# The end of a fused attention and SwiGLU kernel: another order of the last products, halves with a bank each, and stores on two queues

## The chip, the cores and the metric

The kernel runs on one core of one Trainium2 chip. The metric is the device time of one execution in microseconds (us), the median of several runs. Below, TensorE is PE in the profile's rows (PEld its weight loads), VectorE is DVE, ScalarE is ACT, GpSimd is POOL and SyncE is SP; SPq and ACTq are the queues on which SP and ACT issue transfers.

## The reference, cut to what matters

Attention over 8 batches x 8 heads x 576 rows x 64 columns, in float32, with scores below the row's maximum less `tau` masked out, is followed by a SwiGLU block with 512 model columns and 1536 inner columns:

```python
scores = scale * np.matmul(q, k.transpose(0, 1, 3, 2))
thresh = np.max(scores, axis=-1, keepdims=True) - tau
scores = np.where(scores >= thresh, scores, -1000000000.0)
attn = softmax(scores)                       # with 1e-09 added to the sum
x = (attn @ v) as (B*S, H*D)                 # 4608 tokens x 512
g = x @ w_gate                               # 512 x 1536
silu = g * (1.0 / (1.0 + np.exp(-g)))
out = (silu * (x @ w_val)) @ w_out           # 1536 x 512
```

## The kernel before

**Chunks.** The tokens go through the SwiGLU block in chunks of 512. Chunk c, from 0 to 7, holds the first 512 rows of batch c; the 64 rows that are left of each of the 8 batches are gathered into a ninth chunk, c = 8, which the code calls `c == B`. While heads are still being attended, the products of a chunk lie between slots of attention. Chunks 7 and 8 come after the last attention (`tail[0]` is true), and nothing but their own work is left then.

**The output product of a chunk.** A chunk's 512 x 1536 activations times the 1536 x 512 matrix `w_out` is cut 2 x 2 x 2 and done by a scheme of the Strassen family with seven products of (256 x 768) by (768 x 256). Five of them, numbers 0, 1, 3, 5 and 6, are cut the same way once more: `nested` (L1297) issues seven smaller products of three matmuls each. Every float32 matmul stands twice in the profile, so a nested product is 42 matmul records; it lands in two PSUM banks called `px`. Products 4 and 2 are not cut: `flat` (L1314) issues two halves `i` of six matmuls, 24 records in all, both halves into one bank called `py`.

**The four output blocks.** The outcome is a block for each pair (t, e) of token half and column half. A block is 128 partitions x 512 float32 in SBUF, that is two halves `i` of 256 columns. `combine` (L1331) makes a block from a nested product with four DVE instructions. In before there are two places for blocks in the tile `whole`; `n = self.blocks % 2` picks one, and `combine` waits until the earlier store from that place has landed (`*ob_jobs[n]`, L1340). `ship` (L1357) stores a block. For chunk 8 it issues four transfers of 64 KB, all on SP (L1370), one for each half `i` and each 64 partitions `x`, since the rows of one batch are 64 rows of the output.

**The steps of a chunk in the tail** are listed by hand in `Deep.__init__` (L1251):

```python
self.steps = deque([self.p1, self.gates_end, self.p2, self.p7_alone, self.p5, self.p6_alone, self.p3, self.p4_alone])
```

- `p2` makes and ships block (0,0).
- `p7_alone` is nested product 6, copied to SBUF by ACT.
- `p5` is flat product 4. ACT copies its bank to SBUF (L1410), for `corner` needs it.
- `p6_alone` is nested product 5. DVE adds it to an earlier one (`add`, L1480 and L1482), combines what becomes block (0,1), adds `u3`, and `corner` makes and ships block (1,1).
- `p3` is flat product 2, added on top of product 4 in the same bank. One DVE instruction of 128x512 (L1423) adds the bank to block (0,1), which is then shipped.
- `p4_alone` is nested product 3. Two DVE instructions add it (L1480, L1482), `combine` makes block (1,0) from it, and it is shipped last.

**What orders the work around it.** PE's order is that of the calls. DVE, ACT, POOL and SP get their order from a planner (`Plan`): every job has a planned duration, jobs it waits for, and a rank; where several jobs of an engine could start, the lower rank goes first, then the one that was ready first. On the chip each engine runs that list in order. A job of rank 0 is taken ahead of others if it will be ready within 0.2 us. The DVE adds of products have rank 0; in the tail `combine` from SBUF, `u3` and `corner`'s add have rank 1. `take` picks PSUM banks; in the tail there are eight.

Of the kernel before, what the change touches and what calls it, by code (L numbers as in the profile page):

```python
# [14 lines left out]
ALU = mybir.AluOpType  # L15
# [12 lines left out]
class Plan:  # L28
# [12 lines left out]
    def job(self, eng, took, fn, *deps, rank=1, lag=0.0, moves=0.0):  # L41
        j = Job(eng, took, fn, rank, lag, moves)
        for d in deps:
            if isinstance(d, Job) and d.end is None:
                d.then.append(j)
                j.waits += 1
            elif d is not None:
                j.ready = max(j.ready, self.after(d, eng) if isinstance(d, Job) else d + self.HOP)
        if not j.waits:
            self.open[eng].append(j)  # L50
        return j
# [45 lines left out]
    def pe(self, took, fn, *deps):  # L97
        self.force(*deps)
        for d in deps:
            if d is not None:  # L100
                self.t = max(self.t, (d.end if isinstance(d, Job) else d) + self.HOP)
        self.run(self.t)
        fn()
        self.t += took
        return self.t + self.PIPE
# [7 lines left out]
def kernel(  # L113
# [11 lines left out]
    nc = tc.nc  # L125
    P = 128
    B, H, S, D = q.shape
    NP = H // 2
    DM, DFF = w_gate.shape
    NCC = DM // P  # L130
# [7 lines left out]
    SM = 512  # L138
# [4 lines left out]
    TC = 256  # L143
    NU = SM // TC
    BT = TC // (S - SM)
    NF2, DM2 = NF // 2, DM // 2
# [27 lines left out]
    HW = 2 * TC  # L174
# [7 lines left out]
    GW = NQ * HW  # L182
    OW = DM + P
# [586 lines left out]
    def take(name, full=False):  # L770
        free = [b for b in banks if (not b.held if b.fixed is not None else b.n in turns)]
        if full:
            free = [b for b in free if b.full]
            return Hold(min(free, key=Bank.free_at), name) if free else None
        n = sum(b.full for b in free)
        return Hold(min(free, key=lambda b: (b.full and n == 1, max(b.free_at(), plan.t))), name)
# [146 lines left out]
    class Group:  # L923
# [50 lines left out]
        def p6(self):  # L974
            u = self.u1_buf
            if self.b:
                m = self.mul(self.b, self.w[3], xs[1], False, self.cb, *self.w_deps[3], *ready_x[self.c][2])
            else:
                b = self.b = take("pb")
                m = self.mul(b, self.w[3], xs[1], True, *self.w_deps[3], *ready_x[self.c][2], *b.deps)  # L980
                m = job("DVE", 0.7, lambda: nc.vector.tensor_tensor(out=b.rows(), in0=b.rows(), in1=u.ap, op=ALU.add),
                        m, self.s1, rank=0)
                b.bank.full = True
            self.u1 = job("ACT", 0.55, lambda: nc.scalar.activation(u.ap, self.b.rows(), AF.Copy, scale=0.5), m, *self.u1_old, rank=0)
            if self.c >= DEEP and self.g + 2 < NF2:
                load_flow(self.c, self.g + 2, 0, plan.t + plan.PIPE)
# [87 lines left out]
                           (w12, w12, w11, ALU.subtract))[n]  # L1074
            summed.append(job("POOL", 1.3, pool_tt(o[:, fs], x[:, fs], y[:, fs], op), *deps, *summed[-1:], rank=2))

    ob_jobs = [[], []]
    o_of = lambda i, e: ob[:, i, e * DM2:(e + 1) * DM2]

    class Outputs:  # L1080
# [155 lines left out]
    class Deep:  # L1236


        def __init__(self, c, mark):
            self.c = c  # L1240
            halves = [hall[:, t].rearrange("p g f n -> p (g f) n") for t in range(2)]
            self.a11, self.a12, self.a21, self.a22 = (halves[t][:, k * NF2:(k + 1) * NF2] for t in range(2) for k in range(2))
            KW = NF2 * TC
            self.s2, self.s3 = (flow[:, lo:lo + KW].rearrange("p (f n) -> p f n", n=TC) for lo in (GW, GW - KW))
            self.place = flow[:, 0:KW]
            assert GW - KW >= 4 * HW
            self.ready = {}
            self.inner = {}
            self.blocks = 0
            if tail[0]:  # L1250
                self.steps = deque([self.p1, self.gates_end, self.p2, self.p7_alone, self.p5, self.p6_alone, self.p3, self.p4_alone])  # L1251
                self.spaces = [pall[:, n * CW:(n + 1) * CW] for n in range(5)]
            else:
                self.steps = deque([self.p1, self.gates_end, self.p2, self.p5, self.p6, self.p3, self.p7, self.p4])
                self.spaces = [*spaces, None, spaces[1]]
            self.ready["a11"] = [gated[c, 0, x] for x in range(NF2 // 2)]
            self.inner_sums(0, self.a11, self.place, self.ready["a11"], mark)
# [39 lines left out]
        def nested(self, o, holds, first, *deps):  # L1297
# [13 lines left out]
                m = pe(0.67, fn, *ready, *deps, *deep_jobs[o])  # L1311
            return m

        def flat(self, o, a, hold, first, *deps):  # L1314

            for i in range(2):
                def fn(i=i):
                    ps = hold.ap()[:, i * DM2:(i + 1) * DM2]
                    for f in range(NF2):
                        nc.tensor.matmul(ps, a[:, f, i * P:(i + 1) * P], operands[o][:, f, :], start=first and i == f == 0, stop=True,  # L1320
                                         skip_group_check=True)

                m = pe(NF2 * MM, fn, *deps)
            return m

        def copies(self, out, holds, *deps, rank=0):
# [3 lines left out]

        def combine(self, q, *deps, psum=False):  # L1331

            n = self.blocks % 2
            self.blocks += 1
            y = whole.rearrange("p (x q) -> p x q", q=P)
            x, free = n * OW // P, (DM, SPARE)[n] // P
            q0, q1 = (h.ap() for h in q) if psum else (q[:, 0:4 * P], q[:, 4 * P:CW])
            q0, q1 = q0.rearrange("p (x q) -> p x q", q=P), q1.rearrange("p (x q) -> p x q", q=P)
            one = q0[:, 0:1]
            deps = *deps, *ob_jobs[n]  # L1340
            if psum:
                one = y[:, free:free + 1]
                deps = [job("ACT", 0.28, lambda: nc.scalar.copy(one, q0[:, 0:1]), *deps, rank=0)]
                tt, eng, took, less, rank = dve_tt, "DVE", 0.42, 0.29, 0
            else:
                tt, eng, took, less, rank = (dve_tt, "DVE", 0.36, 0.23, 1) if tail[0] else (pool_tt, "POOL", 0.75, 0.44, 2)
            twice = lambda x: x.broadcast_to((P, 2, P))
            j = job(eng, took, tt(y[:, x:x + 2], twice(one), q0[:, 1:3], ALU.add), *deps, rank=rank)
            j = job(eng, took, tt(y[:, x + 3:free + 1:free - x - 3], twice(y[:, x + 1:x + 2]), q1[:, 1:3], ALU.add), j, rank=rank)
            j = job(eng, less, tt(y[:, x + 1], y[:, x + 3], q0[:, 3], ALU.add), j, rank=rank)  # L1350
            j = job(eng, took, tt(y[:, x + 2:x + 4], twice(y[:, free:free + 1]), q1[:, 0:2], ALU.add), j, rank=rank)
            return n, j

        def block(self, n):
            return obs[:, n * OW:n * OW + DM]

        def ship(self, t, e, n, j):  # L1357
            c = self.c
            o = self.block(n).rearrange("p (i n) -> p i n", i=2)
            cols = slice(e * DM2, (e + 1) * DM2)  # L1360

            def fn():
                if c < B:
                    at_ = c * S + t * TC
                    nc.sync.dma_start(out=out[at_:at_ + TC, cols].rearrange("(i p) n -> p i n", p=P), in_=o)
                else:
                    for i in range(2):
                        for x in range(2):
                            r = (t * BT + 2 * i + x) * S + SM
                            nc.sync.dma_start(out=out[r:r + D, cols], in_=o[x * D:(x + 1) * D, i])  # L1370

            ob_jobs[n] = [job("SP", 0.1, fn, j, lag=2.8)]

        def pair(self, name):
            holds = [take(name) for _ in range(2)]
# [30 lines left out]
        def p5(self):  # L1406
# [2 lines left out]
            t = self.spaces[4]  # L1409
            self.c5 = job("ACT", 0.57, lambda: nc.scalar.copy(t[:, 0:DM], y.ap()), m, *u_list[1].jobs, *u_list[2].jobs, *u_list[3].jobs, rank=0)  # L1410

        def p6(self):
            m = self.nested(5, self.x, False, *self.z)
            self.next_flow(0, 0, m)
            self.next_flow(1, 0, m, *self.ready["s4"])
            self.c6 = self.copies(self.spaces[2], self.x, m, *n_list[0].jobs, *n_list[1].jobs)
            self.n12, self.j12 = self.combine(self.spaces[2], *self.c6)
# [19 lines left out]
        def corner(self, t, *deps):  # L1437
            n, j = self.combine(t, *deps)
            o, s = self.block(n), self.spaces[4][:, 0:DM]
            tt, eng, took = (dve_tt, "DVE", 0.62) if tail[0] else (pool_tt, "POOL", 1.3)  # L1440
            j = job(eng, took, tt(o, o, s, ALU.add), j, self.c5, rank=1)
            self.ship(1, 1, n, j)
            for b in u_list:
                b.jobs = [*b.jobs, j]
# [420 lines left out]
```

## Time and profile before

| | us |
|---|---|
| median of 3 runs | 1388.4 (1386.22 to 1389.73) |
| the profiled execution's own time | 1387.66 |
| its span, from the first to the last instruction | 1385.9 |

The span is 1.8 us shorter than the profiled execution's own time, which is 0.7 us below the median of the runs. In the rows a number such as `x12` is a count of instructions; `out<-in` names the tiles written and read; a text in square brackets is the idle time of the engine just before and what ended it. The mean granted clock of TensorE was 0.997.

### The profile page before, as it was taken

How to read it: one execution, taken by the hardware profiler on the slowest of the kernel's cores; microseconds unless marked ns; L12 is line 12 of the kernel's file. 1: busy time of each engine (PE TensorE's matmuls, PEld its weight loads, DVE VectorE, ACT ScalarE, POOL GpSimd, SP SyncE). 2: the span in 40 equal slices, each digit the busy share in tenths (PEclk: the TensorE clock that was granted, in tenths of full speed). 3: DMA queues.
4: the chain of work that ended last, by engine and by line, in shares of the span. 5: the costliest groups of instructions: out<-in, count | busy, mean ns of one | idle time of the engine just before them, and what ended most of it. 6: DMA issues, size and time to landing. Idle time of an engine off the chain costs nothing.

```text
span 1385.9 us, 38809 instructions
## 1 busy us (share of the span) xinstructions
PE 1360.6 (98%) x15486; PEld 1115.8 (81%) x15486; DVE 1024.4 (74%) x2676; ACT 867.0 (63%) x2253; POOL 701.0 (51%) x649
## 2 busy tenths in 40 slices
PE   9998999999999999999999999999999999999997
PEld 6666787778778778878887788888888788899897
DVE  7978888887887776778678777887787764365364
ACT  6887766676756767677777766777677673221220
POOL 2456498844484669534973387427943591000000
PEclk9999999999999999999999999999999999999999
DMA  7834413465523541554154514542255304414411
GB/s 172 217 97 138 101 36 98 124 185 143 172 51 125 145 113 36 169 148 136 36 167 128 148 35 134 154 135 73 78 156 149 97 26 164 160 54 162 141 47 31
DMA packets 208388, 162.30 MB, mean 117 GB/s; under 512 B 166224, under 2 KB 180560, under 8 KB 202832
## 3 DMA queue, kind: packets, MB, share of 16 engines
q1 hardware_dynamic: 204608, 159.39, 40.6%
q8 instruction: 123, 2.02, 0.6%
q10 hardware_dynamic: 3600, 0.43, 0.2%
q14 instruction: 57, 0.47, 0.1%
HBM read 138.28 MB, written 21.50 MB: 115 GB/s over the span
## 4 chain that ended last, share of the span: by engine, by line
PE 90%; DVE 4%; ACT 2%; DMA 1%; SPq 1%; issue 1%; ACTq 0%; DVEq 0%
PE pb L940 17%; PE pa L940 12%; PE pe L940 12%; PE px L1308 12%; PE sc L1514 10%; PE xa L1611 9%; PE po L1106 5%; PE py L1320 5%; PE pg L1040 2%; PE pv L1040 2%; PE sc L940 1%; PE pv L517 1%; SPq L336 1%; DMA vall<-in_v_dram 1%; PE xa L500 1%
## 5 line engine op out<-in xcount | busy, mean ns | idle before, releaser
L1562 DVE SCALAR_TENSOR_TENSOR pall<-sc,th,pall 128x288 f32<-128x288 f32 x504 | 243.7, 514 | 63.7 <-ACT pall L1560 49.5
L940 PE MATMUL pb<-xall,big 128*128 128x256 f32 x1080 | 256.5, 380 | 0.0
L1560 ACT ACTIVATE pall<-sc,nm 128x288 f32<-128x288 f32 x504 | 231.9, 498 | 34.5 <-DVE pall L1562 34.2
L1590 DVE STREAM_TRANSPOSE pall<-pall 128x576 f32<-128x576 f32 x252 | 189.9, 765 | 59.3 <-ACT pall L1588 42.6
L940 PEld LDWEIGHTS pb<-xall,big 128*128 128x128 f32 x1080 | 203.7, 190 | 29.8 <-issue 2.2
L1588 ACT ACTIVATE pall<-pall,ri 128x288 f32<-128x288 f32 x408 | 186.6, 527 | 25.0 <-DVE ri L1576 24.3
L795 POOL TENSOR_TENSOR hall<-hall,tmp 128x512 f32<-128x512 f32 x80 | 103.7, 1296 | 160.1 <-DVE hall L993 144.7
L940 PE MATMUL pa<-xall,big 128*128 128x256 f32 x768 | 183.3, 381 | 0.0
L940 PE MATMUL pe<-xall,big 128*128 128x256 f32 x752 | 178.9, 381 | 0.0
L940 PEld LDWEIGHTS pa<-xall,big 128*128 128x128 f32 x768 | 144.0, 190 | 22.6 <-issue 2.7
L940 PEld LDWEIGHTS pe<-xall,big 128*128 128x128 f32 x752 | 141.9, 190 | 21.5 <-issue 2.7
L1514 PE MATMUL sc<-kT,qT 64*32 64x144 f32 (+1 forms) x5376 | 149.2, 345 | 2.9 <-DVE pall L1562 2.2
L1535 DVE TENSOR_REDUCE mx<-sc 128x2 f32<-128x576 f32 x168 | 124.7, 742 | 26.9 <-PE sc L1514 26.5
L1514 PEld LDWEIGHTS sc<-kT,qT 64*32 64x32 f32 x5376 | 97.8, 106 | 56.4 <-issue 20.2
L1611 PE MATMUL xa<-pall,vall 64*32 64x288 f32 x4032 | 132.3, 404 | 1.0 <-DVE hall L993 0.8
L1585 POOL TENSOR_SCALAR pall<-pall,ri 128x288 f32<-128x288 f32 x96 | 96.0, 1014 | 63.0 <-DVE ri L1576 62.9
L1611 PEld LDWEIGHTS xa<-pall,vall 64*32 64x32 f32 x4032 | 76.4, 107 | 50.1 <-issue 7.2
L1570 ACT COPY sums<-sums 32x6 f32<-32x6 f32 x336 | 66.6, 198 | 45.1 <-DVE pall L1562 40.5
L992 ACT ACTIVATE vall<-tmp 128x512 f32<-128x512 f32 x96 | 60.4, 629 | 52.6 <-DVE tmp L1005 29.9
L1549 ACT COPY mx<-mx 32x6 f32<-32x6 f32 x196 | 38.1, 194 | 61.3 <-DVE mx L1537 59.4
L1320 PE MATMUL py<-wo,hall 128*128 128x256 f32 x336 | 74.8, 379 | 0.0
L1537 DVE TENSOR_REDUCE mx<-sc 128x1 f32<-128x288 f32 x168 | 74.6, 444 | 0.0
(225 smaller groups left out, 2326.2 us busy)
## 6 DMA issues: line engine op xcount, KB each, us to landing
big<-sums_hbm SPq DMA_DIRECT2D x42, 1024.0 KB, 5.2
big<-sums_hbm SPq DMA_DIRECT2D x48, 768.0 KB, 4.7
vall<-in_v_dram SPq DMA_DIRECT2D x112, 144.0 KB, 3.1
out_dram<-big SPq DMA_DIRECT2D x32, 256.0 KB, 3.6
qT<-in_q_dram SPq DMA_DIRECT2D x112, 72.0 KB, 4.7
kT<-in_k_dram SPq DMA_DIRECT2D x112, 72.0 KB, 2.9
wo<-in_moe_w_gate_dram SPq DMA_DIRECT2D x16, 384.0 KB, 3.6
wo<-in_moe_w_val_dram SPq DMA_DIRECT2D x16, 384.0 KB, 4.6
```

The lines of the kernel that those rows point to most:

```text
L795: return lambda: nc.gpsimd.tensor_tensor(out=out, in0=a, in1=b, op=op)
L940: nc.tensor.matmul(ps[:, i], w[:, k_, i * P:(i + 1) * P], x[:, k_, :], start=first and i == k_ == 0, stop=True, skip_group_check=True)
L1308: nc.tensor.matmul(ps, a[:, f, :], ws[n][:, f, :], start=bank_ not in begun, stop=True, skip_group_check=True)
L1320: nc.tensor.matmul(ps, a[:, f, i * P:(i + 1) * P], operands[o][:, f, :], start=first and i == f == 0, stop=True, skip_group_check=True)
L1514: nc.tensor.matmul(pss[h][(slice(g * G, (g + 1) * G), *part)], qT[hs, col:col + G], kT[hs, c * SH + keys[0]:c * SH + keys[1]], start=True, ...
L1535: rs.append(job("DVE", 0.72, lambda n=n, tile_=tile_: nc.vector.tensor_reduce(out=mx[:, n:n + 2, 0], in_=tile_[:, :, 0:SH], axis=AX.X, op= ...
L1560: ej = job("ACT", 0.42, lambda x=x, n=n: nc.scalar.activation(ps[x], scs[x], AF.Exp, bias=nm[:, n:n + 1]), ej, *((masks[h, 0], masks[h, 1] ...
L1562: masks[x] = job("DVE", 0.45, lambda x=x, n=n: nc.vector.scalar_tensor_tensor(out=ps[x], in0=scs[x], scalar=th[:, n:n + 1], in1=ps[x], op0 ...
L1585: scaled.append(job("POOL", 1.02, lambda x=x, n=n: nc.gpsimd.tensor_scalar(out=x, in0=x, scalar1=ri[:, n:n + 1], scalar2=None, op0=ALU.mul ...
L1588: scaled.append(job("ACT", 0.46, lambda x=x, n=n: nc.scalar.activation(x, x, AF.Copy, scale=ri[:, n:n + 1]), rj, rank=rank))
L1590: seg["turned"].append(job("DVE", 0.72, lambda both=both: nc.vector.transpose(out=both, in_=both), *scaled, rank=rank))
L1611: nc.tensor.matmul(holds[a].ap()[x * G:(x + 1) * G, 0:SH].rearrange("d (i q) -> d i q", q=G), vr[rs, h, j, ds], p[rs, h, :, j, :], start=( ...
```

## The change

It concerns chunk 8 alone. The last two steps change places and form: flat product 2, `p3`, now comes last, after `p4_alone`. Both flat products of this chunk are issued as two halves, each half `i` with a PSUM bank of its own (`p5_end`, `p3_end`); ACT copies each half of product 4 by itself, and after product 2 DVE adds and ships each half by itself. Blocks get four places instead of two; the new two lie in the part of `whole` that earlier held streamed weights. A block is stored by two transfers, one for each 64 partitions, one on SP's queue and one on ACT's; the last block has two such pairs, one for each half.

```diff
-    ob_jobs = [[], []]
+    END = (OB + 2 * NCC * DFF + 2 * 3 * HW - GW + NF2 * TC) // P
+    AT_OUT = (0, DM // P), (OW // P, SPARE // P), (END, END + DM // P), (END + OW // P, END + (OW + DM) // P)
+    ob_jobs = [[] for _ in AT_OUT]
...
+                if c == B:
+                    self.steps = deque([self.p1, self.gates_end, self.p2, self.p7_alone, self.p5_end, self.p6_alone, self.p4_alone, self.p3_end])
...
+        def flat_half(self, o, a, i, ps, first, *deps):
+            def fn():
+                for f in range(NF2):
+                    nc.tensor.matmul(ps(), a[:, f, i * P:(i + 1) * P], operands[o][:, f, :], start=first and f == 0, stop=True,
+                                     skip_group_check=True)
+
+            return pe(NF2 * MM, fn, *deps)
...
-            n = self.blocks % 2
+            n = self.blocks % (len(AT_OUT) if self.c == B else 2)
             self.blocks += 1
             y = whole.rearrange("p (x q) -> p x q", q=P)
-            x, free = n * OW // P, (DM, SPARE)[n] // P
+            x, free = AT_OUT[n]
...
         def ship(self, t, e, n, j):
             c = self.c
             o = self.block(n).rearrange("p (i n) -> p i n", i=2)
             cols = slice(e * DM2, (e + 1) * DM2)
+            if c == B:
+                self.ship_end(t, cols, n, o, slice(0, 2), j)
+                return
...
-                    for i in range(2):
-                        for x in range(2):
-                            r = (t * BT + 2 * i + x) * S + SM
-                            nc.sync.dma_start(out=out[r:r + D, cols], in_=o[x * D:(x + 1) * D, i])
...
+        def ship_end(self, t, cols, n, o, i, j):
+
+            ob_jobs[n] = []
+            for x, (eng, queue) in enumerate((("SP", nc.sync), ("ACT", nc.scalar))):
+                to = out.rearrange("(b s) n -> s b n", s=S)[SM:S, t * BT + x:(t + 1) * BT:2, cols]
+                ob_jobs[n].append(job(eng, 0.6, lambda x=x, queue=queue, to=to: queue.dma_start(
+                    out=to[:, i], in_=o[x * D:(x + 1) * D, i]), j, lag=2.0, rank=0))
...
+        def p5_end(self):
+            self.ys = [take("py") for _ in range(2)]
+            t = self.spaces[4]
+            self.c5 = []
+            for i, y in enumerate(self.ys):
+                m = self.flat_half(4, self.a21, i, lambda y=y: y.ap()[:, 0:DM2], True, *y.deps, *self.ready["s1"])
+                self.c5.append(job("ACT", 0.36, lambda i=i, y=y: nc.scalar.copy(t[:, i * DM2:(i + 1) * DM2], y.ap()[:, 0:DM2]),
+                                   m, *u_list[1].jobs, *u_list[2].jobs, *u_list[3].jobs, rank=0))
+
+        def p3_end(self):
+            o = self.block(self.n12).rearrange("p (i n) -> p i n", i=2)
+            for i, y in enumerate(self.ys):
+                m = self.flat_half(2, self.a12, i, lambda y=y: y.ap()[:, 0:DM2], False, self.c5[i], *self.ready["s4"])
+                j = job("DVE", 0.4, lambda i=i, y=y: nc.vector.tensor_tensor(out=o[:, i], in0=y.ap()[:, 0:DM2], in1=o[:, i], op=ALU.add),
+                        m, self.j12, rank=0)
+                self.ship_end(0, slice(DM2, DM), self.n12, o, slice(i, i + 1), j)
+                y.read_by(j)
+                y.done(True)
```

More of the change, by code (lines that the diff above doesn't have):

```diff
@@ L1075, in output_sums @@
             summed.append(job("POOL", 1.3, pool_tt(o[:, fs], x[:, fs], y[:, fs], op), *deps, *summed[-1:], rank=2))
-    ob_jobs = [[], []]
+    END = (OB + 2 * NCC * DFF + 2 * 3 * HW - GW + NF2 * TC) // P
+    AT_OUT = (0, DM // P), (OW // P, SPARE // P), (END, END + DM // P), (END + OW // P, END + (OW + DM) // P)
+    assert NF2 * TC + 2 * OW <= GW and NF2 * TC % P == GW % P == 0
+    ob_jobs = [[] for _ in AT_OUT]
     o_of = lambda i, e: ob[:, i, e * DM2:(e + 1) * DM2]
@@ L1312, in nested @@
             return m
+        def flat_half(self, o, a, i, ps, first, *deps):
[4 more added lines that the diff above has]
+            return pe(NF2 * MM, fn, *deps)
         def flat(self, o, a, hold, first, *deps):
             for i in range(2):
[L1317 to L1323, printed above, removed]
+                m = self.flat_half(o, a, i, lambda i=i: hold.ap()[:, i * DM2:(i + 1) * DM2], first and i == 0, *deps)
             return m
@@ L1354, in block @@
         def block(self, n):
-            return obs[:, n * OW:n * OW + DM]
+            return whole[:, AT_OUT[n][0] * P:AT_OUT[n][0] * P + DM]
         def ship(self, t, e, n, j):
@@ L1360, in ship @@
             cols = slice(e * DM2, (e + 1) * DM2)
+            if c == B:
+                self.ship_end(t, cols, n, o, slice(0, 2), j)
+                return
             def fn():
[L1363 to L1366, printed above, removed]
-                    for i in range(2):
-                        for x in range(2):
-                            r = (t * BT + 2 * i + x) * S + SM
-                            nc.sync.dma_start(out=out[r:r + D, cols], in_=o[x * D:(x + 1) * D, i])
-            ob_jobs[n] = [job("SP", 0.1, fn, j, lag=2.8)]
+                at_ = c * S + t * TC
+                nc.sync.dma_start(out=out[at_:at_ + TC, cols].rearrange("(i p) n -> p i n", p=P), in_=o)
+            ob_jobs[n] = [job("SP", 0.1, fn, j, lag=2.8)]
+        def ship_end(self, t, cols, n, o, i, j):
[4 more added lines that the diff above has]
+                    out=to[:, i], in_=o[x * D:(x + 1) * D, i]), j, lag=2.0, rank=0))
         def pair(self, name):
@@ L1440, in corner @@
             tt, eng, took = (dve_tt, "DVE", 0.62) if tail[0] else (pool_tt, "POOL", 1.3)
-            j = job(eng, took, tt(o, o, s, ALU.add), j, self.c5, rank=1)
+            j = job(eng, took, tt(o, o, s, ALU.add), j, *(self.c5 if self.c == B else [self.c5]), rank=1)
             self.ship(1, 1, n, j)
```

## The prediction

> **What bounds the kernel now.** I read the page first. TensorE is busy for 98% of the span and carries 90% of the chain of work that ended last; its clock digits are nines throughout.
>
> ```profile
> span 1385.9 us, 38809 instructions
> PE 1360.6 (98%) x15486; PEld 1115.8 (81%) x15486; DVE 1024.4 (74%) x2676; ACT 867.0 (63%) x2253; POOL 701.0 (51%) x649
> PE 90%; DVE 4%; ACT 2%; DMA 1%; SPq 1%; issue 1%; ACTq 0%; DVEq 0%
> ```
>
> So the kernel's time is PE's work plus what comes after PE's last product. The change removes no matmul, so only that tail can give anything. The second view is busy time by stretch, with the cuts put where products begin and end (columns: length, PE, PEld, DVE, ACT, POOL, clock, DMA share, GB/s).
>
> ```profile
> 1362.90:1367.60 4.70, 4.70 (x44) 4.70 (x43) 0.00 (x0) 0.59 (x1) 0.00 (x0) 1.00 0.00 0
> 1367.60:1372.70 5.10, 5.10 (x26) 4.51 (x25) 4.80 (x12) 0.00 (x0) 0.00 (x0) 1.00 0.01 3
> 1372.70:1377.60 4.90, 4.89 (x43) 4.67 (x42) 1.15 (x2) 0.00 (x0) 0.00 (x0) 1.00 0.30 68
> 1377.60:1380.50 2.90, 0.00 (x0) 0.00 (x0) 2.20 (x5) 0.00 (x0) 0.00 (x0) 1.00 0.30 66
> 1380.50:1383.00 2.50, 0.00 (x0) 0.00 (x0) 0.42 (x1) 0.00 (x0) 0.00 (x0) 0.50 0.25 57
> 1383.00:1386.00 3.00, 0.00 (x0) 0.00 (x0) 0.00 (x0) 0.00 (x0) 0.00 (x0) 0.50 0.19 43
> ```
>
> To be seen: the last three products (nested 5, flat 2, nested 3) fill PE without a hole up to 1377.6, and then 8.3 us pass without a matmul. ACT does nothing after its copy at 1363. The third view is the timeline of DVE in that tail, the fourth that of SP.
>
> ```profile
> 1377.63 0.69 DVE L1480 TENSOR_TENSOR pall<-px,pall 128x512 f32<-128x512 f32 x1 [3.78 <-PE px L1308]
> 1378.24 0.55 DVE L1482 TENSOR_TENSOR pall<-px,pall 128x384 f32<-128x384 f32 x1
> 1378.70 0.42 DVE L798 TENSOR_TENSOR big<-pall 128x256 f32<-128x256 f32 x1
> 1379.75 1.21 DVE L798 TENSOR_TENSOR big<-big,pall 128x256 f32<-128x256 f32 x3 [0.63 <-DMA out_dram<-big]
> ```
>
> ```profile
> 1380.53 2.38 SPq L1370 DMA_DIRECT2D out_dram<-big  x4
> ```
>
> And of line 1370, the stores of chunk 8, from 1378 on:
>
> ```profile
> L1370 SPq DMA_DIRECT2D out_dram<-big x5: 466/594/596, 1377.6 to 1382.3; - x5
> DMA to landing us min/median/max: 1.9/2.0/2.1
> ```
>
> The 8.3 us are then: 2.90 us from the last product to the first of four stores (two adds, a combine, and 0.63 us in which the combine waits for the store of the block that had its place); 1.8 us until the fourth store is issued at 1382.3, since each takes SP about 0.6; 2.05 us until it lands at about 1384.35; and 1.55 us from there to the end of the span, which is the program's closing and no step of the change touches it. The chain of waits says why the place was late:
>
> ```profile
> 1376.98 0.59 SPq L1370
> 1377.58 0.04 issue
> 1377.62 2.05 DMA out_dram<-big
> 1379.67 0.03 DVEq L798
> ```
>
> Eight stores had queued on SP from 1373.28 (two blocks became ready together), the last went out at 1377.62 and landed at 1379.67.
>
> **The change part by part.** All sums are made against the profiled span of 1385.9.
>
> *Order on PE.* Nested 5, nested 3, flat 2 instead of nested 5, flat 2, nested 3. A nested product is 42 records at 0.112 us, 4.69; a flat one 24 at 0.216, 5.18. Nested 5 starts at 1362.87; nested 3 would then run from 1367.56 to 1372.25 and flat 2 from there, its last matmul starting at 1377.21 and lasting 0.38: 1377.59, as now. Moving costs nothing if the moved product's inputs are early. Nested 3's inner sums end on DVE at 1360.1, 7.4 us before it starts; flat 2 needs ACT's copies of product 4 (the bank was copied at 1363.07) and sums that ended by 1358. Its banks: two `px` are held by nested 5 until DVE has read them (1368.9), two by the `py` halves, which leaves four of eight. If the planner nevertheless gave nested 3 the banks of nested 5, PE would stand until 1368.9, 1.35 us; I take zero.
>
> *After the last product.* Two adds and a four-instruction combine are replaced by one DVE add of 128x256. Rows of that form read 0.42. It starts at 1377.63 and ends at 1378.05; the queues follow a DVE end by 0.03. Half 1 goes out at 1378.08, so 1380.53 - 1378.08 = 2.45 us are gained here, of which 0.63 is the wait for a place.
>
> *The stores.* The last block's second half is two transfers of 64 KB, issued at the same moment by SP and ACT. The three issues that stood before the last store, 1382.3 - 1380.53 = 1.8, are gone. Queued ahead on SP and ACT are block (1,1), ready near 1375, half 0 near 1375.5 and block (1,0) near 1376.6, one issue each of about 0.6: free by 1377.2. An issue of 128 KB (two runs of 1 KB per partition) is in no row of line 1370; the full-chunk stores of 256 KB on SP (L1365) took 0.41, so 0.6 is a safe value; 1.5 us, not seen on this queue, would be needed to hold up half 1.
>
> *What ACT's queue costs.* ACT has issued no transfer since 6.6 us. Its rows there stand beside SP's of the same form: k at 3.2 and 2.7 us to landing on ACTq, 2.8 and 2.5 on SPq, q at 2.9 and 3.1 against 3.2 and 2.6. Thus 0.2 to 0.5 slower at worst. ACT's in-order list has nothing behind these stores that PE or DVE waits for: the first one, of block (0,0) at 1355, has its 0.5 us before the copies at 1357.89, and after the copies of product 4 ACT has nothing but stores.
>
> *A rule against it.* A store of 64 KB lands in 2.0 us, and in the traffic of one such store the DMA digits stand at 9 for 0.3 to 0.4 us: one store fills the engines for that long. The Trainium skill (DMA: Bandwidth & Descriptors, Rules for kernel authors) says not to split a transfer into two over disjoint halves of the partitions, as they go over the same engines and run one after the other. By the row alone the pair lands in 2.05, by the rule in 2.05 + 0.4. I take 2.25 between them. The same page (Issuing engines are not separate DMA queues) adds that several issuers save only issue time, usually small; here issue time is 1.8 of the 8.3 us, so that this rule is no objection to the sum.
>
> *DVE before the end.* After nested 3 (1372.25) DVE still has the last combine step and the add of block (1,1), 1.1; nested 3's two adds, 1.24; its combine, 1.55; half 0's add, 0.42. That is 4.3 us, with hops 4.5, so done near 1376.8, and half 1 is due at 1377.63. So 0.8 us of cover. Were it gone, each us more would show in the end. The split makes two DVE adds of 0.42 from one of 0.68 and two ACT copies of 0.37 from one of 0.59, both hidden under PE. Without the two banks the add of half 0 would have to wait for PE to leave the bank; its store would then be a second one at the end.
>
> *The sum.* 1378.08 + 2.25 + 1.55 = 1381.9 against 1385.9: 4.0 us less. With landing at 2.05 it is 4.2; with 2.6 (rule, and ACT slower by 0.15) it is 3.65. The closing waits on eight transfer semaphores one after another, which may move it by 0.1 either way. The profiled execution (1387.66) is 0.7 below the median shown, and a difference carries over: 1388.4 - 4.0 = **1384.4**.
>
> **The rivals.** *Hidden collisions (part of the gain lost).* PE stands 1.35 us for a bank, or block (1,0) is combined after half 1 has come due and its 256 KB of stores are still in the engines. For it: DVE has only 0.8 us of cover, and two blocks and a half leave within 3.5 us, where before there was one at a time. Against: the bank count, and four stores of before in a row still landed in 2.0 each. It gives 4.0 - 1.35 to 4.0 - 2.0: 1385.8 to 1386.4.
>
> *The new places make waits of their own (the change does not do what it says).* With two places, block (1,0) in the new order would fall on block (0,1), which is not finished then; so the order needs more places, and the new ones overlay streamed weights. If block (1,1) or (1,0) waited there for something, DVE would be held. Against: chunk 8 loads no further weights, and the last product that reads them ends by 1348.5, some 20 us before the first write. A wait of up to 0.8 us would still be covered; one like that of before (0.63) costs nothing, and the time is 1384.4 again.
>
> *Slower: the ACT queue lands late.* Half of the last bytes now depends on a queue that has been idle for 1370 us. Were its landing not 2.25 but above 6.25 us, the whole gain is lost; the longest landing in the trace is 7.3 us (768 KB of weights under full traffic), and at that value the time is 1388.4 - 4.0 + 5.05 = 1389.5. To be slower by 0.3% it needs 10.4. Against: ACTq's own rows of 2.7 to 3.4, and idle engines at the end. I see no reason for it.
>
> **How the numbers follow.** About 0.3% (4.2 us) is what a measurement of this kernel can tell from no change, and my sum lies on that line. The sum as it stands: 0.72. Collisions: 0.20. Slower by the ACT queue or by something not seen: 0.05. Faster than the sum (closing shorter, landing at 2.0): 0.03, inside the range. The runs of before lie 3.5 us apart, so a median of such runs can stray by 1 to 1.5. Range: from 1388.4 - 4.4 - 1.5 = 1382.5 up to the collisions' 1386.4 with 0.6 of scatter, 1387.0. Faster by over 0.3%: somewhat over half of the main case, for its known uncertain terms (closing, landing) lean to the short side, and a little of the others: 0.55. Within: 0.40. Slower: 0.05.
>
> **What would show it.** In the profile after: PE busy to 1377.6 and no later; one DVE add of 128x256 as the last DVE instruction, near 1378.05; the last SPq and ACTq stores start together near 1378.1; landing of the last pair 2.0 to 2.6; no DVE wait on a store; block (1,0)'s stores issued before 1377. A span near 1381.9. Wrong would be: PE idle between nested 5 and nested 3; half 1's add starting later than 0.1 us after PE's end; stores of the last pair landing later than 3 us; or anything that differs before 1354, where the two programs are the same.

## The result and the profile after

The changed kernel took 1383.35 us (median of 6 runs, 1382.15 to 1383.97) against 1388.83 us before (6 runs); the ratio of the two is 0.9963, with a 95% interval of 0.9950 to 0.9976. In a second measurement it was 0.9967 (0.9954 to 0.9979). So it is faster, by about 0.35% (0.2 to 0.5% by the intervals). The profiled execution took 1383.97 us, its span was 1382.1.

Of the page of the changed kernel, the lines that answer to those of before:

```profile
span 1382.1 us, 38805 instructions
PE 1360.9 (98%) x15486; PEld 1115.3 (81%) x15486; DVE 1024.5 (74%) x2677; ACT 867.6 (63%) x2254; POOL 701.2 (51%) x649
PE 91%; DVE 4%; ACT 2%; SPq 1%; DMA 1%; issue 1%; ACTq 0%; DVEq 0%
```

PE does the same work in the same busy time, within 0.3 us. What changed is what follows it. Rows of the timeline of the changed kernel over its last ten microseconds (start, length, engine, line, what it is, and in brackets the idle time before it with what ended it):

```profile
1373.08 5.35 PE L1322 MATMUL py<-wo,hall 128*128 128x256 f32 x24
1375.73 3.67 SPq L1383 DMA_DIRECT2D out_dram<-big  x4
1375.74 3.69 ACTq L1383 DMA_DIRECT2D out_dram<-big  x4
1375.87 0.42 DVE L1437 TENSOR_TENSOR big<-py,big 128x256 f32<-128x256 f32 x1 [0.17 <-PE py L1322]
1376.21 1.20 DVE L798 TENSOR_TENSOR big<-big,pall 128x256 f32<-128x256 f32 x3
1378.46 0.42 DVE L1437 TENSOR_TENSOR big<-py,big 128x256 f32<-128x256 f32 x1 [1.05 <-PE py L1322]
```

The flat product is now last. DVE adds its first half at 1375.87, while PE still works on the second, then finishes block (1,0), and stands idle for 1.05 us before the second half is ready. One add of 0.42 us is all that is left after PE. The last pair of stores, in a narrower window of the same timeline:

```profile
1378.91 0.49 SPq L1383 DMA_DIRECT2D out_dram<-big  x1
1378.92 0.51 ACTq L1383 DMA_DIRECT2D out_dram<-big  x1
```

And the rows of line 1383 from 1378.5 on, with their time to landing:

```profile
L1383 SPq DMA_DIRECT2D out_dram<-big x1: 490/490/490, 1378.9 to 1378.9; - x1
L1383 ACTq DMA_DIRECT2D out_dram<-big x1: 506/506/506, 1378.9 to 1378.9; - x1
DMA to landing us min/median/max: 2.0/2.1/2.2
```

Below, the **tail** of a kernel is the time from the start of the DVE add that waits for the last product to the end of the span: before 1385.88 - 1377.63 = 8.25 us, after 1382.10 - 1378.46 = 3.64 us. It is 4.6 us shorter, although the span is only 3.8 us shorter: DVE's add, and with it the end of PE's work, lies 0.83 us later in this execution than in that of before. That has nothing to do with the change. The two programs are alike up to 1354, and the last product ahead of that, the last one of the SwiGLU gates, is late by as much already. Its row before, and its row after:

```profile
1346.58 1.89 PE L940 MATMUL sc<-xall,big 128*128 128x256 f32 x8
1347.41 1.89 PE L940 MATMUL sc<-xall,big 128*128 128x256 f32 x8
```

From there to the add it is 31.05 us in both, and in every other trace too, but for 31.2 in three parts (below). Of the 0.83 us, 0.29 stem from the transfer that brings `tau` in: it ended DVE's first wait at 5.50 us here and at 5.21 there. Where the rest arose was not looked for. The add starts anywhere from 1376.1 to 1379.6 us in the executions profiled here. This is why the tail, and not the span, is compared below. The 4.6 us are 2.45 from the end of PE's work to the first of the last stores, 1.79 of issues on SP, and 0.55 of the closing after the last landing, less 0.16 for a later landing.

### The profile page after: what moved, and what is told of

Its sections match the earlier page's. It is cut to its first block, busy times and chain, and to the rows that moved or that the text cites. A ratio compares the mean times of both kernels' runs of the same rounds, so it can differ in the third digit from the quotient of the medians.

```text
span 1382.1 us, 38805 instructions
## 1 busy us (share of the span) xinstructions
PE 1360.9 (98%) x15486; PEld 1115.3 (81%) x15486; DVE 1024.5 (74%) x2677; ACT 867.6 (63%) x2254; POOL 701.2 (51%) x649
## 4 chain that ended last, share of the span: by engine, by line
PE 91%; DVE 4%; ACT 2%; SPq 1%; DMA 1%; issue 1%; ACTq 0%; DVEq 0%
PE pb L940 17%; PE pa L940 12%; PE pe L940 12%; PE px L1313 12%; PE sc L1545 10%; PE xa L1642 9%; PE po L1109 5%; PE py L1322 5%; PE pg L1040 2%; PE pv L1040 2%; PE sc L940 1%; PE pv L517 1%; SPq L336 1%; PE xa L500 1%; PE sc L1313 1%
```

## The experiments

The question was which of the parts (order, halves with a bank each, two queues, four places) earns how much, and whether the parts add up. The theory was: the late combine, the wait for a place and the series of issues on SP are separate terms of the tail. The rivals were: one part carries it all, or two stores side by side gain nothing, since they go over the same engines.

**Two queues alone.** The kernel before, with this in `ship` for chunk 8:

```diff
+            if c == B:
+                for x, (eng, queue) in enumerate((("SP", nc.sync), ("ACT", nc.scalar))):
...
+                        out=to, in_=o[x * D:(x + 1) * D]), j, lag=2.0, rank=0))
```

> The kernel before, with only the stores of chunk 8 changed to two a block, one on SP's queue and one on ACT's; old order, one bank, two places. I read the tail: from the start of the DVE add that waits for the last product to the end of the span, 8.25 us before and 3.6 after. Theory (the series of issues and the late combine are separate terms): the issues, 1.8, go; the queue is no longer backed up, so the block's place is free in time and the 0.63 of waiting goes as well, although there are still two places; the last pair has 256 KB and lands some 0.6 later than 64 KB did. Tail 5.7 to 6.3, about 2.2 us less. Rival (the pair runs one after the other on the same engines, so nothing but issue time is saved, and the wait for the place stays): 6.9 or more. Rival (the stores are the whole gain, the order adds nothing): tail 3.6 to 4.2.

Measured: ratio 0.9995 (0.9987 to 1.0004). Its timeline at the end:

```profile
1379.64 0.69 DVE L1482 TENSOR_TENSOR pall<-px,pall 128x512 f32<-128x512 f32 x1 [3.78 <-PE px L1308]
1380.25 0.55 DVE L1484 TENSOR_TENSOR pall<-px,pall 128x384 f32<-128x384 f32 x1
1380.71 0.41 DVE L798 TENSOR_TENSOR big<-pall 128x256 f32<-128x256 f32 x1
1381.16 1.21 DVE L798 TENSOR_TENSOR big<-big,pall 128x256 f32<-128x256 f32 x3
1382.40 0.60 SPq L1366 DMA_DIRECT2D out_dram<-big  x1
1382.40 0.64 ACTq L1366 DMA_DIRECT2D out_dram<-big  x1
```

The wait on a store is gone from DVE, with two places, as the theory had it: the stores of the earlier blocks left in time. But the tail is 1386.31 - 1379.64 = 6.67 us, more than expected. The terms that the theory names, 8.25 - 1.8 - 0.63 + 0.6, come to 6.4 already, so its range was too low. One thing had been left out: a pair carries both halves of a block, and so waits for the last DVE step (until 1382.37), where the first of the four stores of before needed only one half and left 0.43 us ahead of that step's end. And ACT's half of a pair of 256 KB landed after 2.9 us in the two earlier pairs of this run, 0.2 more than allowed (the landing of the last one is not in the trace; SP's took 2.5). Against that, the closing was some 0.4 us shorter; the section on the prediction comes back to this. The rival of 6.9 is nearer to this number than the theory, but its wait for a place is refuted.

**Places alone.** The kernel before, with `AT_OUT` and four places:

```diff
-            n = self.blocks % 2
+            n = self.blocks % (len(AT_OUT) if self.c == B else 2)
-            x, free = n * OW // P, (DM, SPARE)[n] // P
+            x, free = AT_OUT[n]
```

> The kernel before, with only four places for the blocks of chunk 8 instead of two. Theory: the wait of 0.63 us of the last combine for its place goes and nothing else: tail 7.6 instead of 8.25; SP's queue is empty again by 1378.2, before the first store at 1379.9, so that the gain is not lost there. Rival (the store queue only takes the wait over): 8.25. In the times 0.6 us cannot be told from nothing.

Measured: ratio 0.9996 (0.9987 to 1.0005), tail 1384.51 - 1376.87 = 7.64. The timeline:

```profile
1376.87 0.69 DVE L1483 TENSOR_TENSOR pall<-px,pall 128x512 f32<-128x512 f32 x1 [3.78 <-PE px L1311]
1377.95 0.41 DVE L798 TENSOR_TENSOR big<-pall 128x256 f32<-128x256 f32 x1
1378.40 1.21 DVE L798 TENSOR_TENSOR big<-big,pall 128x256 f32<-128x256 f32 x3
```

No bracket stands behind the last row: the wait is gone, the tail is 0.61 us shorter, and nothing took the wait's place.

**Order alone.** The changed kernel with `p5` and `p3` whole, as before, and four stores a block on SP. It keeps the four places, which the new order needs:

```diff
-... self.p5_end, self.p6_alone, self.p4_alone, self.p3_end])
+... self.p5, self.p6_alone, self.p4_alone, self.p3])
...
+                for i in range(2):
+                    for x in range(2):
+                        nc.sync.dma_start(out=out[r:r + D, cols], in_=o[x * D:(x + 1) * D, i])
```

> The changed kernel with the flat product last, but with its two halves in one bank, one DVE add of 128x512 for the whole block, and four stores of 64 KB a block on SP as before. Theory: the add and combine of 2.9 us shrink to 0.7, but three blocks become ready within 3.5 us and SP needs 0.64 for each of their twelve stores, so the last store is issued near 4.3 us after the last product instead of 4.7; tail 7.2 to 7.8. Rival (the order alone is worth its shorter work on DVE): 8.25 - 2.2 = 6.0 or less.

Measured: ratio 0.9996 (0.9987 to 1.0005), tail 1385.31 - 1377.60 = 7.71. The timelines of SP and of DVE:

```profile
1374.87 7.49 SPq L1384 DMA_DIRECT2D out_dram<-big  x12
1377.60 0.69 DVE L1456 TENSOR_TENSOR big<-py,big 128x512 f32<-128x512 f32 x1 [1.64 <-PE py L1322]
```

DVE is done 0.69 us after PE, and SP goes on issuing until 1382.36, twelve stores in one row without a gap. The work taken away after PE was replaced by a queue. The order by itself, with its places, is worth 0.5 us.

**Old order with all the rest.** The changed kernel with the last two steps changed back:

```diff
-... self.p6_alone, self.p4_alone, self.p3_end])
+... self.p6_alone, self.p3_end, self.p4_alone])
```

> The changed kernel with the old order of the last two steps: halves with a bank each, four places and two queues stay, the nested product comes last again. Theory: without the order the halves and places are worth nothing, since the block that leaves last is the nested product's; tail as with the two queues alone, 5.7 to 6.3. Rival (halves with a bank each help by themselves): below 5.2.

Measured: ratio 0.9987 (0.9978 to 0.9996), tail 1385.09 - 1378.54 = 6.55. Rows of the timeline:

```profile
1378.54 0.69 DVE L1511 TENSOR_TENSOR pall<-px,pall 128x512 f32<-128x512 f32 x1 [3.66 <-PE px L1313]
1380.06 1.21 DVE L798 TENSOR_TENSOR big<-big,pall 128x256 f32<-128x256 f32 x3
1381.30 0.62 SPq L1383 DMA_DIRECT2D out_dram<-big  x1
1381.30 0.66 ACTq L1383 DMA_DIRECT2D out_dram<-big  x1
```

From the first add to the pair it is 2.76 us, as with two queues alone, and the tail is the same within 0.12 us, as expected; the range of 5.7 to 6.3 was missed for the same reasons. Halves and places earn next to nothing where the nested product comes last.

**One queue.** The changed kernel with both stores of a pair on SP:

```diff
-            for x, (eng, queue) in enumerate((("SP", nc.sync), ("ACT", nc.scalar))):
+            for x, (eng, queue) in enumerate((("SP", nc.sync), ("SP", nc.sync))):
```

> The changed kernel with both stores of a pair on SP's queue; the order, the halves with a bank each and the places stay. Tail of the changed kernel: 3.6 us from the last DVE add to the end. Theory (issue time counts, and SP is the bottleneck of the last 3.5 us): eight stores of some 0.62 each become ready within 3.2 us, so SP still has one and a half ahead of the last pair; the second of it goes out 1.6 to 1.7 us after the add starts... plus 0.5, so that the tail is 4.6 to 5.2. Rival (only the second issue of the last pair counts): 4.1 to 4.2. Rival (a second queue saves nothing that matters): 3.6 to 3.8. For the closing: if it is 1.5 us again, as in the three kernels with all stores on SP, and not 0.96 to 1.07 as with two queues, then it goes with the queues.

Measured: ratio 0.9974 (0.9965 to 0.9984), tail 1381.43 - 1376.60 = 4.83. The timeline:

```profile
1376.50 2.58 SPq L1383 DMA_DIRECT2D out_dram<-big  x4
1376.60 0.42 DVE L1437 TENSOR_TENSOR big<-py,big 128x256 f32<-128x256 f32 x1 [1.05 <-PE py L1322]
```

SP is still at the stores of block (1,0) when the last half is ready at 1377.02. It comes to that half at 1377.88, over 0.8 us later, and is done issuing at 1379.08. The second queue is worth 4.83 - 3.64 = 1.2 us, which is more than the one issue that it takes over in the last pair.

**Whole banks.** The changed kernel with both flat products whole, both halves in one bank, and one pair of stores for the last block (the steps of order alone, the stores of the changed kernel).

> The changed kernel with the flat products whole: both halves in one bank, one ACT copy, one DVE add of 128x512 at the end, and one pair of stores of 128 KB each for that block. Theory: the add is 0.69 instead of 0.42, and the pair carries 256 KB, which landed in 2.5 and 2.85 us where two queues alone were tried and in 2.8 in the changed kernel; so the tail is 0.3 + 0.6 longer, 4.4 to 4.6. Rival (halves save DVE time alone): 3.9. Rival (256 KB for the last block collide with those of block (1,0) besides): 4.9 or more.

Measured: ratio 0.9973 (0.9963 to 0.9984), tail 1381.34 - 1376.68 = 4.66. The timeline:

```profile
1376.68 0.69 DVE L1454 TENSOR_TENSOR big<-py,big 128x512 f32<-128x512 f32 x1 [1.63 <-PE py L1322]
1377.40 0.60 SPq L1383 DMA_DIRECT2D out_dram<-big  x1
1377.40 0.63 ACTq L1383 DMA_DIRECT2D out_dram<-big  x1
```

That is just above the 4.4 to 4.6 of the theory and below the 4.9 of the collision. The halves are worth 1.0 us: 0.27 on DVE, 0.64 because the last pair is half as large (ACT's half landed 2.85 us after issue instead of 2.21), and 0.1 in the closing.

**The last half without ACT's store, and without SP's.** In each, one of the last two stores is left out:

```diff
             for x, (eng, queue) in enumerate((("SP", nc.sync), ("ACT", nc.scalar))):
+                if i == slice(1, 2) and x:            # or: and not x
+                    continue
```

> The changed kernel without ACT's store of the last half: 64 rows of each of two batches in a quarter of the columns are not written. It shows the last SP store alone. In the changed kernel the pair landed 1.96 (SP) and 2.21 us (ACT) after issue. Theory (the two share the engines, and the second pays for the first): SP's still lands in 1.95, the tail is 0.25 shorter, 3.35 to 3.4. Rival (each slows the other): SP's lands in 1.6 to 1.8. Rival (ACT's queue itself is slow): SP's in 1.95 too; the next run separates these.

> The changed kernel without SP's store of the last half: 64 rows of each of two batches in a quarter of the columns are not written. ACT's store then goes out alone. With both, ACT's landed 2.21 us after issue and SP's, alone or not, 1.94 to 1.96. If ACT's own queue is the slower one, it lands in 2.2 again and the tail stays 3.6; if it was late only because it shares the engines with SP's, it lands in 1.95 and the tail is 3.35 to 3.4.

Measured, of line 1385 without ACT's store from 1378.5 on:

```profile
L1385 SPq DMA_DIRECT2D out_dram<-big x1: 490/490/490, 1378.8 to 1378.8; - x1
DMA to landing us min/median/max: 1.9/1.9/1.9
```

and without SP's, from 1376.3 on:

```profile
L1385 ACTq DMA_DIRECT2D out_dram<-big x1: 496/496/496, 1376.6 to 1376.6; - x1
DMA to landing us min/median/max: 2.0/2.0/2.0
```

The tails are 1381.75 - 1378.38 = 3.37 and 1379.50 - 1376.12 = 3.38. Either store alone lands in 1.9 to 2.0 us. So ACT's queue by itself is not the slower one. In the pair, ACT's store, which starts 5 ns behind SP's, pays 0.25 us for the company, and SP's pays nothing.

**Queues changed over.** The changed kernel with ACT for partitions 0 to 63 and SP for 64 to 127.

> The changed kernel with the queues of a pair changed over: partitions 0 to 63 by ACT, 64 to 127 by SP. In the changed kernel ACT's store of each pair landed 0.2 to 0.3 us after SP's, in each of the four pairs. If that goes with ACT's queue, ACT's stays later by as much; if it goes with the partitions or with which is named first in the program, SP's is now the later one. Tail 3.6 in both cases.

Measured: SP's store of the last half landed in 2.0 us and ACT's in 2.2, tail 1381.11 - 1377.48 = 3.63. So the delay does not go with the partitions. It does not go with the order in the program either, which was changed over too: ACT's issue still started 5 ns after SP's. ACT's was the later one of the pair in every run, so whether it pays because it is second, or because it is ACT's beside SP's, these runs do not tell apart.

**Again, and in three parts.** The second kernel cuts the second half into two quarters of 128 columns with a bank each:

```diff
+        PARTS = (0, slice(0, DM2)), (1, slice(0, P)), (1, slice(P, DM2))
...
-            for i, y in enumerate(self.ys):
+            for (i, cs), y in zip(self.PARTS, self.ys):
```

> The changed kernel as it is, for a closer ratio and beside the next one. Theory: the tail is 8.25 - 3.63 = 4.6 us shorter, and nothing else differs; ratio 0.9967, within 0.996 to 0.9975, and a tail of 3.6 again. Rival (the 5.5 us between the medians are more than the tail, so that something before it gained too): ratio 0.9955 or less.

> The changed kernel with both flat products in three parts and three banks: the first half, and the second half in two quarters of 128 columns, each with its own add and pair of stores of 32 KB. Theory: the last add is 0.29 instead of 0.42, the last pair half as large; PE pays some 0.05 for narrower matmuls; tail 3.3 to 3.5, which the times cannot show. Rival (the landing is a fixed delay and more stores only crowd the queues): 3.6 or more.

Measured: the changed kernel again 0.9967 (0.9954 to 0.9979), tail 1380.82 - 1377.19 = 3.63, as expected; the rival's 0.9955 lies at the very edge of the interval. Three parts 0.9970 (0.9960 to 0.9979). Its timeline:

```profile
1377.31 1.23 SPq L1383 DMA_DIRECT2D out_dram<-big  x2
1377.36 1.46 ACTq L1383 DMA_DIRECT2D out_dram<-big  x2
1377.73 0.29 DVE L1439 TENSOR_TENSOR big<-sc,big 128x128 f32<-128x128 f32 x1 [0.94 <-PE sc L1322]
```

The tail is 1381.06 - 1377.73 = 3.33, as expected, 0.3 us shorter. The flat product runs from 1372.26 to the add, 5.47 us, against 5.38 in the changed kernel, so that 0.2 us remain, and the times do not show them. ACT now issues the last store 0.2 us after SP, for it is busy with the one before. This finer cut is not worth taking.

**All together.** A tail that is shorter by so much should shorten the time by as much; the last column is 1 - (8.25 - tail) / 1388.8:

| kernel | tail, us | measured ratio | ratio from the tail |
|---|---|---|---|
| before | 8.25 | 1 | 1 |
| order alone | 7.71 | 0.9996 | 0.9996 |
| places alone | 7.64 | 0.9996 | 0.9996 |
| two queues alone | 6.67 | 0.9995 | 0.9989 |
| old order, all the rest | 6.55 | 0.9987 | 0.9988 |
| changed, one queue | 4.83 | 0.9974 | 0.9975 |
| changed, whole banks | 4.66 | 0.9973 | 0.9974 |
| changed | 3.64 | 0.9963, 0.9967 | 0.9967 |
| changed, three parts | 3.33 | 0.9970 | 0.9965 |

Every value from a tail lies in the interval of the measured one, which reaches 0.001 (1.4 us) to each side. So within that the tail is the whole gain; the equal 31.05 us ahead of it say the same more sharply. And the parts do not add up: order (with its places), places and queues, each alone, save 0.54, 0.61 and 1.58, at most 2.7 together, while the change saves 4.6. Of the 1.58 of the two queues, 0.4 is the shorter closing. The order alone is worth 0.5, but with the stores in pairs and the halves it is worth 6.55 - 3.64 = 2.9, because the queue no longer takes back what DVE gives. What the places are worth inside the changed kernel was not measured, since the order needs them.

## Why the prediction was right

- *PE's order costs nothing.* Right. PE has no hole; the flat product takes 5.35 us, 5.34 before.
- *One add after the last product, 0.42, and a hop of 0.03.* Right: 1378.46 plus 0.42 and the issue at 1378.91. Of the 2.45 us that this step was to save, 0.63 was the wait for a place, and places alone showed 0.61.
- *The queues are free in time.* Right, with an issue of 128 KB at 0.6 us. One queue showed that it is no small matter: with both stores of a pair on SP they were not free.
- *DVE has cover of 0.8 us.* It had 1.05.
- *The landing, taken at 2.25 between 2.05 and 2.45.* 2.2 was measured. The 2.25 was a midpoint between two theories and not worked out, so there is some luck in the match. Of the 0.4 us that the rule on two transfers over halves of the partitions (the Trainium skill, DMA: Bandwidth & Descriptors, Rules for kernel authors) would have added, 0.25 are there, and they come from the pair's company and not from ACT's queue alone, for which the upper bound had allowed 0.15. The same page says that several issuers save issue time alone, which is usually small (Issuing engines are not separate DMA queues); here it was 1.2 us of the tail, against one queue with the same stores. Whether one transfer of all 128 partitions, which the rule advises, would have done as well as the pair, no run here shows.
- *The closing, 1.55 us after the last landing, which no step of the change touches.* This term was mis-sized, and its reason was wrong. It measured 1.51 us before and 1382.1 - 1381.13 = 0.96 after, and this is most of the difference between the 4.0 us of the sum and the 4.6 us of the profile. In the closing SP waits for the last stores to complete and then runs three instructions named DRAIN. Their rows (shortest, median and longest in ns, then the first and the last start) in before, in order alone and in the changed kernel:

```profile
L1860 SPq DRAIN  x3: 7/7/130, 1385.0 to 1385.4; - x3
L1893 SPq DRAIN  x3: 7/7/130, 1384.1 to 1384.9; - x3
L1891 SPq DRAIN  x3: 7/7/7, 1381.3 to 1381.6; - x3
```

One DRAIN of before takes 130 ns, and SP stands still for 0.34 us ahead of it, where the changed kernel has 0.04: 0.43 us in all. In before and in places alone it is the first DRAIN, in order alone the second, but in all three it is the 848th instruction of SP in the trace. In every trace SP pauses like this ahead of every 128th of its instructions from the 80th on, for 0.34 to 0.45 us. The other kernels end at 837 to 845 instructions of SP and never come to the 848th; the changed kernel has 840 where before had 852. So fewer instructions on SP moved the pause out of the closing, and not the second queue (with one queue the closing was 0.90) nor the order. What SP does in the pause, no run shows. The other 0.1 of the 0.55 is one wait fewer for a store after the last landing, and that much the prediction had allowed. The change did not aim at the 0.43: that the gain came out above the sum is luck.
- *The rivals.* No PE stop and no collision showed, the new places made no wait, and ACT's queue landed at 2.2 us, not at 6.25.

The forecast of 1384.4 was 1.05 us above the measured median; 0.55 of that is the closing, and the rest is within the scatter of medians.

## What to carry to other kernels

At the end of a program, order the last work so that the least follows it: what counts is the path from the last product to the last landing, not the number of instructions. Look at the store queue together with it, for a queue of small stores can give back all that a shorter path gains, as it did with the order alone. Two changes that each measure as nothing can be worth several microseconds together, so judge them by the term that they shorten, read in the profile, and not one by one by the measured time. When the end of a program is read that closely, look into the closing as well: a few instructions fewer on a queue were worth 0.4 us here.

## What the runs showed of the hardware

Stores of 64 KB left one queue every 0.63 us (twelve in a row, order alone) and each still landed in 1.9 to 2.1 us, so a row of them cost issue time and not landing time. Of two stores of 64 KB issued within 5 ns on two queues, SP's landed in 1.96 us as it did alone, and ACT's in 2.21 instead of 1.96; of 128 KB each, the last pairs landed in 2.5 to 2.6 us on SP and 2.8 to 2.9 on ACT. SP stood still for 0.34 to 0.45 us ahead of every 128th of its instructions, in all thirteen traces; in three of them one such pause fell into the closing, behind the last landing, and made it 1.5 us long instead of 0.8 to 1.1.
